# Turning part B's input once in part A and fetching the turned images later: one change to a two-part attention kernel

## Chip, cores and metric

The kernel runs on one core of a Trainium2 chip. The metric is the device time of one execution in microseconds. A core has five engines that run side by side and meet through semaphores: TensorE (PE; its weight loads are shown as PEld), VectorE (DVE), ScalarE (ACT), GpSimd (POOL) and SyncE (SP). SyncE computes nothing here: it issues transfers, one after the other, and a transfer whose semaphore isn't there yet holds up all that stand behind it on SyncE. GpSimd issues some transfers as well. All transfers are carried out by the core's 16 DMA engines.

## What is computed

Two independent parts, both bf16, whose outputs stand side by side in the last dimension. Part A is a sliding attention in which each token looks at 8 tokens, 2 apart. Part B is a recurrence over 64 segments of 32 tokens: each segment attends over 8 memory rows and its own 32 rows, and the first 8 rows of its output are the memory of the next.

```python
def _A_ref(x, wqkv, wo):                    # x (1, 2048, 640), H = 32, Dh = 20
    qkv = (x @ wqkv).reshape(B, S, 3, H, Dh)
    idx = pos[:, None] - arange(8) * 2      # masked where < 0
    logits = einsum('bhsd,bhswd->bhsw', q, k[idx]) * Dh ** -0.5
    o = einsum('bhsw,bhswd->bhsd', softmax(logits), v[idx])
    return o.reshape(B, S, D) @ wo

def _B_ref(x, mem0, Wq, Wk, Wv, Wo, seg_len):   # x (1, 2048, 640), H = 32, Dh = 192, M = 8
    mem = mem0
    for s in range(64):
        h = concatenate([mem, x[:, 32 * s:32 * s + 32]], axis=1)    # 40 rows
        q, k, v = h @ Wq, h @ Wk, h @ Wv                            # per head
        p = softmax(where(mask, q k^T * Dh ** -0.5, -1e9))
        o = einsum('bhte,hed->btd', p v, Wo)
        mem = o[:, :8]
        outs.append(o[:, 8:])
    return concatenate(outs, axis=1)
```

## The kernel before

The two parts run one after the other on TensorE. While part A computes, SyncE loads and copies what part B will need.

**Part A** (`part_a`, L24) works in blocks of 512 tokens for the projections and of 256 tokens for the attention. `turn_x(s)` (L47) lets a transposing transfer lay the s-th block of 512 tokens into `xT`, of which there are two buffers: the transfers for blocks 0 and 1 start at once, block 2 needs the buffer of block 0, block 3 that of block 1. `step(b, fill)` (L178) does the attention of a 256-token block; the projections of the next 512-token block are woven into it (`more`, `group`). Steps 2 and 3 project block 2, steps 4 and 5 block 3. The order of TensorE, VectorE and ScalarE is written out by hand in part A (`manual_schedule`, L234); for SyncE and GpSimd the compiler's scheduler places the instructions, by and large in the order of the text. `output` (L166) stores a result by way of two `ob` buffers, from GpSimd for the first two blocks and from SyncE for the rest (L176). `turn_x(3)` stands at the end of step 1 in the text (L229).

**The loads ahead** (`emit_loads`, L358) are issued by SyncE within part A, in this order: `turn_x(1)`; 37 pieces of part B's weights that stay on the chip (`load_resident`, L326, 320 or 384 KB each); `turn_x(2)`; 23 pieces that don't fit and are copied from their input into a contiguous DRAM tile each (`copy_streamed`, L295); and the copies of x into windows (`copy_windows`, L339).

**The windows.** A segment's TensorE input is 64 columns wide: 32 main columns (8 of memory, which are written over later, and the segment's first 24 tokens), and 32 columns "ahead", the last 8 tokens of each of four segments. `XW` (L337) is a DRAM tile of 64 windows of 64 rows of 640 values, so each token row is copied into the right windows: 26 transfers. In part B `load_x(s)` (L425) turns window s by one transposing transfer into `HX` (128 partitions x 5 x 64), one of two buffers.

**Part B** (`part_b`, L272; `segment`, L594) goes through four groups of 8 heads: projections q, k, v (`project32`, L435), scores, softmax, mixing with v, and the output projection `project_out` (L570). `get_unit` (L387) hands out a weight piece: a resident one, or a streamed one, for which SyncE issues a load from the DRAM copy into one of five `ws` buffers (shown as `t`). Each segment streams the same 23 pieces, in the order k0 (2), k1 (2), v0 (2), k2 (2), v1 (1), o0 (2), k3 (2), v2 (1), o1 (3), v3 (1), o2 (2), o3 (3). Nine further resident pieces (`early`) are loaded when part A frees their memory, and the last 15 (`wait`) when segment 0 first asks for them. At the end of a segment `memory_rows` (L582) writes the new memory into the first columns of the next HX. TensorE's order in part B is written by hand (L655), SyncE's is the scheduler's.

## Time and profile before

Three runs took 2023.1, 2030.83 and 2033.13 us; the median is 2030.83. The profiled execution is one more.

| What | Value |
|---|---|
| profiled execution, its time | 2024.66 us |
| its span, first to last instruction | 2022.8 us |
| part A, until TensorE's first work for part B | 0 to 176.3 us |
| segment 0 | 176.3 to 217 us |
| segments 1 to 62, by the memory rows | 28.6 us each in the mean |
| TensorE busy, 217 to 1990 us | 1727.68 of 1773.00 us |
| DMA share, 0 to 100 us; 100 to 145; 145 to 180; 180 to 217 | 1.02; 0.22; 0.57; 0.98 |
| HX, transposing load | 64 issues, median 1.2 us of SyncE, 4.4 us to landing |
| streamed pieces | 64 x 23 loads, 4.3 to 4.8 us to landing |

How to read it: an engine's line gives the microseconds in which it was busy, merged; "idle before, releaser" says how long it stood and what ended the wait. A matmul's end is modelled, so a TensorE that is shown busy may still be waiting a little. SyncE's instructions are issues; what is told of them is the start, the time that SyncE was held, and the time to landing. The granted clock is the share of TensorE's full speed; 0.5 means that it ran at half speed. The DMA share is the part of the 16 engines' time that packets took, and can lie a little over 1.

### The profile page before, as it was taken

The numbers are of one execution on the slowest core, as the hardware profiler recorded it, in microseconds if no ns is written. First come the engines' busy times: TensorE is split into PE (matmuls) and PEld (weight loads), VectorE is DVE, ScalarE is ACT, GpSimd is POOL, SyncE is SP. The second block draws the span as 40 slices with busy tenths as digits, with TensorE's granted clock in tenths as the row PEclk, the third lists the DMA queues.
The fourth block names the chain that finished last, engine by engine and source line by source line (L and its number), as shares of the span: only waits on it lengthen the run. The fifth ranks groups of instructions, "written<-read, shape, count | busy, mean of one in ns | idle before, by whom it ended". The sixth has DMA issues, their size and how long they took to land.

```text
span 2022.8 us, 97144 instructions
## 1 busy us (share of the span) xinstructions
PE 1945.4 (96%) x42512; PEld 1243.6 (61%) x42512; DVE 1128.3 (56%) x3622; ACT 725.6 (36%) x2126; POOL 193.6 (10%) x674
## 2 busy tenths in 40 slices
PE   7989999999999999999999999999999999999998
PEld 4656666666666666666666666666666665666665
DVE  5875555555555455555555555555555554555554
ACT  3543333333333333333333333333333333333333
POOL 2000000110001101001001001101001001110110
PEclk9999999999999999999999999999999999999999
DMA  9927999999899999999999989999899988989997
GB/s 343 311 76 269 311 300 305 301 302 307 290 305 304 299 288 312 302 304 303 303 299 297 308 292 311 305 303 299 296 298 303 298 304 284 303 293 300 305 302 257
DMA packets 270123, 596.29 MB, mean 295 GB/s; under 512 B 61065, under 2 KB 72841, under 8 KB 269385
## 3 DMA queue, kind: packets, MB, share of 16 engines
q1 hardware_dynamic: 264770, 585.97, 87.9%
q8 instruction: 333, 5.46, 1.1%
q0 software_dynamic: 4928, 4.11, 0.6%
q14 instruction: 92, 0.75, 0.1%
HBM read 576.85 MB, written 18.87 MB: 295 GB/s over the span
## 4 chain that ended last, share of the span: by engine, by line
PE 71%; DMA 19%; DVE 6%; ACT 1%; issue 1%; SPq 1%; POOL 0%; DVEq 0%; POOLq 0%; ACTq 0%
PE acc L443 33%; PE Y L578 18%; DMA t<-wcopy_k 8%; DMA t<-wcopy_o 6%; PE pt L456 6%; PE Sps L515 4%; PE OTps L564 4%; PE pq L95 2%; PE pt L547 2%; DVE sb L423 2%; DMA out_dram<-row 2%; DMA t<-wcopy_v 1%; PE po L161 1%; DMA wcopy_o<-in_B_Wo_dram 1%; PE py L172 1%
## 5 line engine op out<-in xcount | busy, mean ns | idle before, releaser
L443 PEld LDWEIGHTS <-HX 128*32 128x32 bf16 x19380 | 462.7, 96 | 274.3 <-issue 46.5
L578 PEld LDWEIGHTS <-OT 128*64 128x64 bf16 x6144 | 316.8, 109 | 131.0 <-ACT OT L423 20.0
L578 PE MATMUL Y<-wres_o,OT 128*64 128x320 bf16 x3584 | 344.3, 302 | 2.2
L443 PE MATMUL acc<-wres_q,HX 128*32 128x384 bf16 x6460 | 332.6, 328 | 0.5 <-ACT sb L423 0.2
L443 PE MATMUL acc<-t,HX 128*32 128x384 bf16 x4200 | 309.1, 328 | 12.9 <-DMA t<-wcopy_k 10.1
L578 PE MATMUL Y<-t,OT 128*64 128x320 bf16 x2560 | 277.7, 303 | 10.0 <-DMA t<-wcopy_o 9.2
L423 DVE CAST sb<-acc 128x384 bf16<-128x384 f32 x322 | 178.8, 556 | 186.6 <-PE acc L443 171.3
L443 PE MATMUL acc<-wres_v,HX 128*32 128x384 bf16 x4844 | 276.5, 328 | 0.1
L528 ACT ACTIVATE t<-t 128x160 f32<-128x160 f32 x256 | 86.1, 336 | 439.4 <-DVE t L527 439.4
L443 PE MATMUL acc<-wres_k,HX 128*32 128x384 bf16 x3876 | 224.8, 327 | 0.3 <-issue 0.3
L522 DVE SCALAR_TENSOR_TENSOR t<-Sps,mask 128x160 f32<-128x160 f32 x256 | 82.8, 323 | 214.6 <-PE Sps L515 186.6
L423 ACT CAST sb<-acc 128x384 bf16<-128x384 f32 x324 | 153.6, 474 | 125.1 <-PE acc L443 123.5
L456 PE MATMUL pt<-ident,sb 128*128 128x128 bf16 x1938 | 179.4, 221 | 6.9 <-DVE sb L423 1.7
L423 DVE CAST OT<-OTps 128x120 bf16<-128x120 f32 x512 | 125.5, 271 | 97.4 <-PE OTps L564 96.8
L488 POOL COPY QT<-Lb 128x96 bf16<-128x96 bf16 x252 | 67.4, 267 | 1112.0 <-PE Sps L515 955.2
L456 PEld LDWEIGHTS <-sb 128*128 128x128 bf16 x1938 | 110.2, 97 | 82.3 <-issue 32.3
L515 PEld LDWEIGHTS <-QT 128*64 128x64 bf16 (+1 forms) x4096 | 118.9, 109 | 55.1 <-issue 40.5
L423 ACT CAST OT<-OTps 128x120 bf16<-128x120 f32 x512 | 106.0, 258 | 110.7 <-PE OTps L564 110.4
L515 PE MATMUL Sps<-KT,QT 128*64 128x40 bf16 (+1 forms) x4096 | 137.0, 188 | 2.2 <-DVE KT L423 1.0
L530 DVE TENSOR_REDUCE sm<-t 128x4 f32<-128x160 f32 x256 | 81.8, 320 | 78.7 <-ACT t L528 78.7
L564 PEld LDWEIGHTS <-Vst 32*128 32x128 bf16 (+1 forms) x4096 | 62.2, 97 | 82.3 <-issue 60.5
L564 PE MATMUL OTps<-PT,Vst 32*128 32x40 bf16 (+1 forms) x4096 | 109.7, 192 | 0.0
(75 smaller groups left out, 1916.0 us busy)
## 6 DMA issues: line engine op xcount, KB each, us to landing
t<-wcopy_o SPq DMA_DIRECT2D x640, 320.0 KB, 4.3
t<-wcopy_k SPq DMA_DIRECT2D x512, 384.0 KB, 4.8
t<-wcopy_v SPq DMA_DIRECT2D x320, 384.0 KB, 4.8
wres_q<-in_B_Wq_dram SPq DMA_DIRECT2D x20, 384.0 KB, 7.7
wres_v<-in_B_Wv_dram SPq DMA_DIRECT2D x15, 384.0 KB, 7.8
wres_k<-in_B_Wk_dram SPq DMA_DIRECT2D x12, 384.0 KB, 7.7
wres_o<-in_B_Wo_dram SPq DMA_DIRECT2D x14, 320.0 KB, 6.7
wcopy_o<-in_B_Wo_dram SPq DMA_DIRECT2D x10, 320.0 KB, 8.1
```

What stands on the lines that cost most here:

```text
L95: nc.tensor.matmul(pq[32 * d:32 * d + 32], lhsT=wcol[:, k, t, 4 * c + d, :], rhs=xTs[s][:, k, :], start=(k == 0), stop=(k == 4), tile_posi ...
L423: (nc.scalar.copy if copies["n"] % 2 else nc.vector.tensor_copy)(dst, src)
L443: nc.tensor.matmul(ps[n][32 * j:32 * j + 32, :], lhsT=X[:, dc, :], rhs=w[:, 384 * j:384 * j + 384], start=(dc == 0), stop=(dc == 4), tile_ ...
L456: nc.tensor.matmul(pt[:, c], lhsT=sb[:, 128 * c:128 * c + 128], rhs=ident, start=True, stop=True)
L488: nc.gpsimd.tensor_copy(tokens(T)[:, :, 32:L], b[:])
L515: nc.tensor.matmul(Sps[64 * g2:64 * g2 + 64, a, :], lhsT=QT[lo:hi, L * cc:L * cc + 64], rhs=KTt[lo:hi, cc, :], start=(g2 not in seen), sto ...
L522: nc.vector.scalar_tensor_tensor(out=t1[:], in0=Sps[:], scalar=scale, in1=mask[:].unsqueeze(1).to_broadcast([128, 4, L]), op0=ALU.mult, op ...
L528: nc.scalar.activation(t1[:], t1[:], ACTF.Exp)
L530: nc.vector.tensor_reduce(out=sm[:], in_=t1[:], axis=AX.X, op=ALU.add)
L547: nc.tensor.transpose(pt[:, late, :], P[:, late].rearrange("p a n -> p (a n)"), ident)
L564: nc.tensor.matmul(dst, lhsT=V[32 * a:32 * a + 32, e0:e1], rhs=PT[32 * a:32 * a + 32, late, half, :], start=(wide and late == 0 and half = ...
L578: nc.tensor.matmul(Y[64 * gv:64 * gv + 64, :], lhsT=OT[:, L * c:L * c + 64], rhs=w[:, n:n + 320], start=(i == 0 and r == 0), stop=(i == 23 ...
```

## The change

1. The windows are grouped by sets of four segments (`XW` becomes 16 x 64 rows x 4 segments x 640), and all their copies (32 transfers) go to the front of SyncE's queue, right behind `turn_x(1)`.
2. After `turn_x(3)`, at the end of step 1, `rest` issues 16 transposing transfers, each of which turns four windows at once into a stage, and GpSimd stores the stage into four images in DRAM (`XT`, 128 rows of 640 B for each segment). The four stages lie in the memory of the four resident v1 pieces, which are loaded behind that; `copy_streamed` now follows the transposes.
3. `load_x(s)` is a plain load of an image. It moves from the start of `segment` to behind the values of group 1.
4. SyncE's order in part B is that of the text (`manual_schedule` takes SP in).
5. In segment 0, from the sixth streamed piece on, each streamed load is preceded by the load of one of the 15 waiting resident pieces.
6. All outputs of part A are stored by GpSimd.

```diff
-    emit_loads(turn_x)
+    rest = emit_loads(turn_x)
...
-        (nc.sync if b > 1 else nc.gpsimd).dma_start(out2[r0:r0 + 128, 0:D], ob[:])
+        nc.gpsimd.dma_start(out2[r0:r0 + 128, 0:D], ob[:])
...
         if b == 1:
             turn_x(3)
+            rest()
...
-    XW = dpool.tile([n_seg, 2 * SEG, Dm], BF16, name="xwindows")
+    n_sets = n_seg // 4
+    XW = dpool.tile([n_sets, 2 * SEG, 4, Dm], BF16, name="xwindows")
+    XT = dpool.tile([n_seg, 128, 5 * 2 * SEG], BF16, name="ximages")
...
+    def turn_images(stage):
+
+        for b in range(n_sets):
+            part = stage[b % len(stage)]
+            nc.sync.dma_start_transpose(part, XW[b].rearrange("n s d -> n (s d)"))
+            nc.gpsimd.dma_start(XT[4 * b:4 * b + 4].rearrange("s p n -> p s n"),
+                                part.rearrange("p (s c) n -> p s (c n)", s=4))
+
     def emit_loads(turn_x):
         turn_x(1)
-        load_resident(resident[:n_pre], [nc.sync])
+        copy_windows()
+        last = [u for u in resident[:n_pre] if u[:2] == ("v", 1)]
+        load_resident([u for u in resident[:n_pre] if u not in last], [nc.sync])
         turn_x(2)
-        copy_streamed()
-        copy_windows()
+
+        def rest():
+            wide = joined["v", 1][0][:].rearrange("p n c -> p (n c)")
+            turn_images([wide[:, 1280 * i:1280 * i + 1280].rearrange("p (c n) -> p c n", n=2 * SEG) for i in range(4)])
+            copy_streamed()
+            load_resident(last, [nc.sync])
+
+        return rest
...
+    ahead_of = []
+
     def get_unit(u):
...
+        if wait:
+            ahead_of.append(u)
+            if len(ahead_of) > nbuf:
+                v = next(v for v in resident if v in wait)
+                wait.remove(v)
+                load_resident([v], [nc.sync])
         t = wstream.tile([128, SLOT], BF16, tag="ws")
...
     def load_x(s):
         if s < n_seg:
-            nc.sync.dma_start_transpose(HXs[s % 2][:], XW[s])
+            nc.sync.dma_start(HXs[s % 2][:].rearrange("p c n -> p (c n)"), XT[s])
...
     def segment(s):
         last = s + 1 == n_seg
-        load_x(s + 1)
...
         V[1] = values(s, 1)
+        load_x(s + 1)
...
-    with tc.manual_schedule(engines={mybir.EngineType.PE}):
+    with tc.manual_schedule(engines={mybir.EngineType.PE, mybir.EngineType.SP}):
```

More of the change, by code (lines that the diff above doesn't have):

```diff
@@ L320, in unit_tile @@
         return v.rearrange("p (k d) -> p k d", k=2) if u[0] == "o" else v
+    joined = {("v", 1): []}
     def place_resident(pool, units):
         for u in units:
-            res[u] = pool.tile([128, unit_cols(u)], BF16, name="wres_%s%d_%d" % u)[:]
+            part = joined.get(u[:2])
+            if part is None:
+                res[u] = pool.tile([128, unit_cols(u)], BF16, name="wres_%s%d_%d" % u)[:]
+                continue
+            if not part:
+                n = sum(v[:2] == u[:2] for v in units)
+                part.append(pool.tile([128, n, 1536], BF16, name="wres_%s%d" % u[:2]))
+            res[u] = part[0][:, sum(v[:2] == u[:2] for v in res), :]
     def load_resident(units, engs):
@@ L336, in part_b @@
     dpool = ctx.enter_context(tc.tile_pool(name="b_copy", bufs=1, space=bass.MemoryType.DRAM))
-    XW = dpool.tile([n_seg, 2 * SEG, Dm], BF16, name="xwindows")
+    n_sets = n_seg // 4
+    XW = dpool.tile([n_sets, 2 * SEG, 4, Dm], BF16, name="xwindows")
+    XT = dpool.tile([n_seg, 128, 5 * 2 * SEG], BF16, name="ximages")
     def copy_windows():
-        rows = [(XW[0, 0:M], mem2[0:M]), (XW[0, M:SEG], x2[0:SEG - M])]
-        for a, b in ((1, 49), (49, n_seg)):
-            rows.append((XW[a:b, 0:SEG], x2[SEG * a - M:SEG * b - M].rearrange("(s n) d -> s n d", n=SEG)))
-        groups = x2.rearrange("(t n) d -> t n d", n=SEG)[:, SEG - M:SEG]
-        groups = groups.rearrange("(m k) n d -> k m n d", k=4)
-        windows = XW[:].rearrange("(m k) n d -> k m n d", k=4)
-        for r in range(4):
+        rows = [(XW[0, 0:M, 0], mem2[0:M]), (XW[0, M:SEG, 0], x2[0:SEG - M])]
+        sets = x2.rearrange("(m r n) d -> r m n d", r=4, n=SEG)
+        for r in range(4):
+            lo = 1 if r == 0 else 0
+            own = x2[4 * SEG * lo + SEG * r - M:]
+            span = 4 * SEG * (n_sets - 1 - lo)
+            rows.append((XW[lo:n_sets - 1, 0:SEG, r],
+                         own[0:span].rearrange("(m q) d -> m q d", q=4 * SEG)[:, 0:SEG]))
+            rows.append((XW[n_sets - 1, 0:SEG, r], own[span:span + SEG]))
@@ L348, in copy_windows @@
             for i in range(4):
-                dst = windows[r][:, SEG + M * i:SEG + M * i + M]
+                dst, src = XW[:, SEG + M * i:SEG + M * i + M, r], sets[i][:, SEG - M:SEG]
                 if i >= r:
-                    rows.append((dst, groups[i]))
+                    rows.append((dst, src))
                 else:
-                    rows.append((dst[0:n_seg // 4 - 1], groups[i][1:n_seg // 4]))
-                    rows.append((dst[n_seg // 4 - 1], groups[i][n_seg // 4 - 1]))
+                    rows.append((dst[0:n_sets - 1], src[1:n_sets]))
+                    rows.append((dst[n_sets - 1], src[n_sets - 1]))
```

## The prediction

> **What bounds the kernel now.** I read the page's totals and slices first, then who waits for whom, then SyncE's queue in part A, then the microseconds around one transposing load in part B.

> ```profile
> span 2022.8 us, 97144 instructions
> PE 1945.4 (96%) x42512; PEld 1243.6 (61%) x42512; DVE 1128.3 (56%) x3622; ACT 725.6 (36%) x2126; POOL 193.6 (10%) x674
> DMA  9927999999899999999999989999899988989997
> ```

> TensorE is busy for 96% and the DMA engines for 0.9 nearly everywhere; the hole in the third and fourth slices (101 to 202 us) is the second half of part A. So TensorE sets the time, and what can be won is its idle time and what it loses when it restarts. The waits of TensorE:

> ```profile
> PE acc L443 <- DMA t<-wcopy_k: 10.1, 32, 0.9
> PE Y L578 <- DMA t<-wcopy_o: 9.2, 23, 0.8
> PE pt L547 <- DVE P L540: 6.1, 23, 0.7
> PE pq L95 <- DMA xT<-in_A_x_dram: 5.9, 1, 5.9
> PE acc L443 <- DMA t<-wcopy_v: 1.1, 4, 0.4
> ```

> (us in total, times, longest.) 20.4 us in 59 waits go to streamed weights over the whole of part B (21.5 us in 70, where waits of 60 to 150 ns are counted too), and 5.9 us to one late transpose in part A. A matmul of L443 takes 328 ns (the page's group) and the next is issued 41 ns later (20 in 0.82 us), so a wait that shows as idle has hidden some 0.28 us more while the pipeline drained: 59 x 0.28 = 16.5, in all 37 us. Segments run 27.8 to 31.2 us, 28.6 in the mean.

> SyncE's queue in part A (start, duration) and the restart of TensorE:

> ```profile
> 16.00 3.88 SPq L328 DMA_DIRECT2D wres_q<-in_B_Wq_dram  x5
> 48.08 1.32 SPq L328 DMA_DIRECT2D wres_q<-in_B_Wq_dram  x2
> 50.13 6.59 SPq L49 DMA_TRANSPOSE xT<-in_A_x_dram  x1
> 82.34 24.57 SPq L356 DMA_DIRECT2D xwindows<-in_B_x_dram  x25
> 107.02 2.98 SPq L49 DMA_TRANSPOSE xT<-in_A_x_dram  x1
> ```
> ```profile
> 70.19 1.09 PE L95 MATMUL pq<-xT,a_wq 128*32 128x512 bf16 x16
> 112.15 2.37 PE L95 MATMUL pq<-xT,a_wq 128*32 128x512 bf16 x20 [5.89 <-DMA xT<-in_A_x_dram]
> ```

> The four blocks of A's x (L49) are turned by SyncE. The fourth is issued at 107.0 only because 25 window copies stand ahead of it, and TensorE stands for it. The third, issued at 50.1 behind the resident pieces, is in time: its first use is the line at 70.19.

> Around the load of HX at 1009.25 (columns: busy and count of each engine, granted clock, DMA share, GB/s):

> ```profile
> 1010.00:1011.00 1.00, 1.00 (x16) 0.48 (x10) 0.24 (x1) 0.00 (x0) 0.12 (x1) 1.00 0.97 370
> 1011.00:1012.00 1.00, 1.00 (x48) 0.55 (x44) 0.29 (x2) 0.27 (x2) 0.00 (x0) 1.00 0.78 239
> 1012.00:1013.00 1.00, 1.00 (x22) 0.74 (x16) 0.18 (x1) 0.15 (x1) 0.00 (x0) 1.00 1.35 123
> 1013.00:1014.00 1.00, 0.90 (x14) 0.55 (x10) 0.00 (x0) 0.00 (x0) 0.00 (x0) 1.00 0.49 115
> ```

> While the transpose runs, the stream falls from about 300 to 120 GB/s. Averaged over the segments' loads it is 215 and 164 GB/s in the third and fourth us after the issue: (85 + 136) KB missing, 0.74 us of stream a segment. It hits the k pieces with which the next segment begins.

> **The sum, part by part.**

> *Transposing load out, plain load in.* Removed: 64 transposes, 1.2 us of SyncE each (median row) and the 0.74 us of stream. Added: 128 rows of 640 B; packets of 640 B took 32 to 35 ns in part A, 128/16 x 34 ns = 0.27 us. The k waits it causes are those in the first 7 us of a segment: 16 waits, 3.8 us, with the drain 3.8 + 16 x 0.28 = 8.3. I take them as gone. The out_dram rows of a segment travel in the same first microseconds, when the stream catches up at 350 to 360 GB/s, and VectorE waits for them (14.6 us, 12 times), which passes to TensorE as part of the 6.1 us above: I take 2 of it. Against that, the 0.27 us now lie between v1 and o0, some 8 us ahead of k3, the tightest place (26 waits, 8.1 us, at 14 to 17 us into the segment). At worst every such segment moves by 0.27, 26 x 0.27 = 7; SyncE is waiting for free slots there, so I take 1.3. Body: -8.3 - 2 + 1.3 = **-9**, bounds +7 (no gain, full price) and -37 (every stream wait goes with it).

> *Windows first in part A, two transposes.* The fourth block no longer waits for the windows: -5.9, and -1.4 for the 2.9 us of work at half clock that follow (granted clock 0.50 from 112.2 to 115): -7.3. The third block now stands behind 32 window copies instead of none, and behind 33 resident pieces instead of 37. Pieces go at 0.98 us (37 from 16.0 to 50.1, less a short start). Window copies: 15 of them took 0.75 us each once nothing held them (95.6 to 106.9), the median issue is 0.56; the DMA time of 4096 rows of 1280 B at 62 ns is 4096/16 x 62 = 16 us. So 16 to 24, I take 21. The block's packets start at 16 + 21 + 33 x 0.98 = 69.3 and need 4 us to land: 73.3 against 70.2, a stall of 3.1 and 1 us of half clock: +4, bounds 0 and +8. Sum for A: **-3.3**.

> *Sixteen transposes and stores.* On the DMA engines: 1280 packets of 256 B at 20.7 ns, 1.66 us each, 26.5 in all; stores of 512 packets of 640 B, 1.1 each, 17.4. Room: the share was 0.22 from 100 to 145 and 0.57 from 145 to 180, so 35 + 15 = 50 us are free for 44. On SyncE one costs some 2 us (1.19 for 320 packets, 2.98 for 2560). A stage is reused after transpose and store: 4 to land, 1 to issue, 5 to 6 to land (out_dram from POOL at 80 us: 5.8), over four stages 2.6 us each: 80 + 16 x 2.6 = 122. Then 23 streamed copies (56.8 to 81.2 before: 24 us), 4 v1 pieces, HX and 9 early pieces, 14 us: done by about 160, and part B begins near 173. Cost nothing; the cover is 13 us, and without it each us late is a us of TensorE.

> *Outputs of A to POOL.* 12 issues of 0.54 us. SyncE waited 50.5 us for ScalarE's ob; now POOL does, and the image stores behind it. Two ob buffers give a step (18 us) of grace: nothing.

> *SyncE in program order; pieces ahead in segment 0.* Around 1009 to 1037 SyncE already issues the 23 pieces in program order: nothing. From 180 to 217 the DMA share is 0.98, but TensorE waits 1.1 us there in all. Fifteen pieces of 1 us placed earlier: -1.1 to +3, I take **-0.5**.

> Sum: -9 - 3.3 - 0.5 = -12.8. The profiled execution took 2024.66 us (span 2022.8, 1.9 around it); it would become 2011.9. It lies 6.2 under the median of the three runs, 2030.83, from which I count: **2018**.

> **Rivals.**

> *The tail of part A is late (slower).* One mechanism: the four stages. If transposes land as under backlog (10.2 us, the third block) and stores at 8.5 (POOL at 63 us), one takes (10.2 + 1 + 8.5)/4 = 4.9 us, 16 take 79: done at 159, the streamed copies at 183, HX and the first k after 188 to 197 instead of 173: +15 to +24, with the body's -9 and A's -3.3 about 2030.8 + 19.5 - 12 = **2038**. It decides from (173 - 38 - 80)/16 = 3.4 us per transpose. For it: stores may queue on POOL behind outputs. Against it: the engines are free there, and outputs of 160 KB landed in 1.8 us after 120.
> VectorE's products in part A take 1.22 us each, and POOL's issues beside them 0.54 us with 5.8 us to land at 80 us; whether any of that is VectorE's doing can't be told from the full queue. [...]

> *The ring of five slots is the limit (same).* k0's slot is freed by o14 of the segment before; if the late k pieces come from that and not from the transpose, the waits at 14 to 17 and at 26 us stay and the first ones too, and only A's -3.3 and a little remain: **2027**. For it: 54 of the 70 waits lie more than 7 us into a segment. Against it: the fall to 120 GB/s.

> *All stream waits are one chain (faster).* If the catching up is what makes the later pieces late as well, 37 us go: **1992**. For it: after the fall the stream runs at 350 to 400 GB/s, with no reserve. Against it: by 8 us into the segment it is back at 300.

> **How the numbers follow.** Chances: my forecast 0.42, all waits 0.15, the ring 0.20, the late tail 0.23. Less than 0.5% (10 us) can't be told from no change, since the three runs span 10 us. The forecast's own range is 2008 to 2026, of which I put 0.30 beyond 10 us and 0.12 within; of the ring 0.03 faster, 0.15 same and 0.02 slower; of the tail 0.21 slower, 0.02 same; all waits is faster. So faster 0.48, same 0.29, slower 0.23. The range reaches into both outer cases, 1994 to 2046: it leaves out about half of all waits and a fourth of the tail.

> **What would show it.** Right: no wait of L95 for xT at 112; no fall of GB/s in the last 6 us of a segment; waits for wcopy_k in the first 7 us gone, segments of 28.5 us in the mean. Wrong: a wait of L95 near 70 of over 8 us; SyncE still in its transposes after 135, or L443 waiting at its first matmuls; k3's waits grown by more than the first ones shrank; or a stream that still falls at the plain load.

## The result, and the profile after

The changed kernel takes 2044.59 us (median of six runs, 2043.22 to 2056.21); the kernel before, timed beside it, 2027.12 (six runs, 2017.82 to 2033.13). The ratio is 1.0105 with a 95% interval of 1.0068 to 1.0141: slower by about 1%. The profiled execution took 2044.17 us, its span is 2042.4, 19.6 more than before.

| What | Before | After | Difference |
|---|---|---|---|
| span | 2022.8 | 2042.4 | +19.6 |
| TensorE's first work for part B | 176.3 | 193.4 | +17.1 |
| first memory rows (end of segment 0) | 217.2 | 235.3 | +18.1 |
| segments 1 to 62, mean of one | 28.601 | 28.597 | 0.00 |

So 17.1 of the 19.6 us are lost in part A; segment 0 adds 1.0, and the end behind the last memory rows 1.8. The segments, for which the change was forecast to win 9 us, show no difference. (The mean of one profile is uncertain by about 0.1 us a segment: in e4 below, which leaves part B as it was before, it is 28.72.) The page's totals and slices after:

```profile
span 2042.4 us, 97154 instructions
PE 1948.3 (95%) x42512; PEld 1248.8 (61%) x42512; DVE 1127.1 (55%) x3622; ACT 726.8 (36%) x2126; POOL 212.0 (10%) x702
DMA  8995999999999998999999989989989998989997
```

The hole of the DMA engines, two slices before (101 to 202 us), is now the fourth slice alone (153 to 204): the new transposes fill most of it, as they should. TensorE is busy for 2.9 us more and idle for some 17 more. Its waits (us in total, times, longest):

```profile
PE pq L95 <- DMA xT<-in_A_x_dram: 10.3, 1, 10.3
PE Y L616 <- DMA t<-wcopy_o: 9.6, 22, 2.2
...
PE py L172 <- ACT ob L174: 7.9, 1, 7.9
PE acc L481 <- DMA t<-wcopy_k: 7.4, 15, 1.4
...
PE acc L481 <- DMA t<-wcopy_v: 4.5, 10, 1.0
```

The wait for xT has not gone, it has become longer; a wait of 7.9 us is new; the streamed weights come to 21.5 us, 20.4 before. Both long waits, in TensorE's timeline:

```profile
72.07 0.39 PE L145 MATMUL pr<-P,a_repm 32*128 32x512 bf16 x2
82.79 1.51 PE L95 MATMUL pq<-xT,a_wq 128*32 128x512 bf16 x12 [10.33 <-DMA xT<-in_A_x_dram]
...
139.33 1.49 PE L172 MATMUL py<-a_wo,ao 128*128 128x320 bf16 x5 [7.93 <-ACT ob L174]
```

**The first wait** is for the third block of A's x. SyncE's timeline (start, how long SyncE was held, how many) shows what stood ahead of it:

```profile
16.65 0.86 SPq L370 DMA_DIRECT2D xwindows<-in_B_mem_dram  x1
17.56 25.28 SPq L370 DMA_DIRECT2D xwindows<-in_B_x_dram  x31
42.88 2.48 SPq L338 DMA_DIRECT2D wres_q<-in_B_Wq_dram  x5
...
72.12 1.21 SPq L338 DMA_DIRECT2D wres_q<-in_B_Wq_dram  x2
74.05 9.35 SPq L49 DMA_TRANSPOSE xT<-in_A_x_dram  x2
83.44 6.61 SPq L376 DMA_TRANSPOSE wres_v<-xwindows  x4
```

The windows hold SyncE for 26.2 us (16.65 to 42.84), the 33 pieces until 73.3, and only at 74.05 is the third block's transpose issued. Even then most of its packets don't start: the pieces were issued ahead of the engines (the one of 72.1 lands at 79.3), and the block's own packets, a few from 77.5 on, go mostly from 80 to 82.7.

**The second wait** is for an output buffer. GpSimd's and ScalarE's timelines:

```profile
130.86 0.75 POOL L377 DMA_DIRECT2D ximages<-wres_v  x1 [1.77 <-DMA wres_v<-xwindows]
131.61 1.10 POOL L176 DMA_DIRECT2D out_dram<-ob  x2
139.90 0.54 POOL L176 DMA_DIRECT2D out_dram<-ob  x1 [7.20 <-ACT ob L174]
```
```profile
138.85 1.08 ACT L174 CAST ob<-py 128x320 bf16<-128x320 f32 x3 [8.34 <-DMA out_dram<-ob]
```

The two results of block 2 lay ready in their buffers at 113.9 and 115.2. The scheduler had put their stores behind the last image store on GpSimd, and an image store waits for its transpose (50.6 us in 13 waits between 84 and 142). So they were issued at 131.6 and 132.2, and the first landed at 138.8; until then ScalarE had no buffer for block 3, and TensorE no place for its next product.

**Half clock after each.** In windows around the two waits (length; busy and count of PE, PEld, DVE, ACT, POOL; granted clock; DMA share; GB/s) the clock stays at half speed when the matmuls run again:

```profile
72.00:83.00 11.00, 0.67 (x8) 0.43 (x10) 3.08 (x3) 1.66 (x5) 0.00 (x0) 0.61 1.13 287
83.00:88.00 5.00, 5.00 (x46) 1.88 (x42) 1.23 (x1) 1.66 (x3) 0.00 (x0) 0.50 1.16 223
139.00:142.70 3.70, 3.37 (x17) 1.93 (x20) 0.13 (x1) 1.50 (x5) 1.08 (x2) 0.51 1.04 327
```

It is at half from 74.4 to 88.0 and from 135.8 to 142.7. Work at half takes twice as long (the 20 matmuls of L95 take 2.36 us from 82.8 and 1.25 us from 88.3), so (88.0 - 82.8)/2 = 2.6 and (142.7 - 139.3)/2 = 1.7 us are lost. Part A then adds up: 10.3 + 2.6 + 7.9 + 1.7 = 22.5, less the 7.3 of the fourth block's old stall, plus 2.2 that were lost ahead of 72 us (0.8 in the start, 1.4 because a stretch at half clock from 33.4 us lasted 6.8 us where it was 3.4): 17.4, where 17.1 were measured.

**Part B.** The fall of the stream that the prediction saw is gone. The four microseconds before segment 28, at the place of the transposing load before:

```profile
998.00:999.00 1.00, 1.00 (x44) 0.64 (x46) 0.00 (x0) 0.29 (x1) 0.12 (x1) 1.00 0.99 296
999.00:1000.00 1.00, 1.00 (x20) 0.56 (x22) 0.47 (x2) 0.42 (x2) 0.00 (x0) 1.00 0.85 280
1000.00:1001.00 1.00, 1.00 (x18) 0.84 (x16) 0.00 (x0) 0.00 (x0) 0.00 (x0) 1.00 0.93 273
1001.00:1002.00 1.00, 0.92 (x16) 0.26 (x12) 0.16 (x1) 0.43 (x1) 0.00 (x0) 1.00 0.96 336
```

273 to 336 GB/s, where it fell to 115. Over all segments the two lowest microseconds rose from 225 and 136 GB/s to 260 and 301. Yet the waits for weights in the first 7 us of a segment are 3.5 us in 12, from 3.8 in 16. The stream is smoother and the pieces are as late as they were, only in other places. Of the waits over 150 ns, those for k in the first 7 us fell from 2.6 us in 9 to 1.0 in 3 and those for v there rose from 0.7 in 3 to 2.2 in 6. For o0, which now comes right behind the plain load (7 to 14 us into a segment), they rose from 0.7 us in 2 to 5.4 in 9, and for k3 (14 to 18 us) they fell from 7.5 in 23 to 4.3 in 9.

### The profile page after: what moved, and what is told of

It is laid out like the page before. It is cut to its first block, busy times and chain, and to the rows that moved or that the text cites. A ratio compares the mean times of both kernels' runs of the same rounds, so it can differ in the third digit from the quotient of the medians.

```text
span 2042.4 us, 97154 instructions
## 1 busy us (share of the span) xinstructions
PE 1948.3 (95%) x42512; PEld 1248.8 (61%) x42512; DVE 1127.1 (55%) x3622; ACT 726.8 (36%) x2126; POOL 212.0 (10%) x702
## 4 chain that ended last, share of the span: by engine, by line
PE 69%; DMA 20%; DVE 6%; SPq 2%; issue 2%; ACT 1%; POOL 0%; DVEq 0%; POOLq 0%; ACTq 0%
PE acc L481 32%; PE Y L616 19%; DMA t<-wcopy_o 7%; PE pt L494 6%; DMA t<-wcopy_k 5%; PE Sps L553 4%; PE OTps L602 4%; DMA out_dram<-row 2%; PE pt L585 2%; DMA t<-wcopy_v 2%; DVE sb L461 2%; DMA wres_v<-xwindows 1%; SPq L370 1%; SPq L49 1%; DMA ximages<-wres_v 1%
## 5 line engine op out<-in xcount | busy, mean ns | idle before, releaser
L481 PEld LDWEIGHTS <-HX 128*32 128x32 bf16 x19380 | 463.2, 96 | 272.7 <-issue 46.0
L616 PEld LDWEIGHTS <-OT 128*64 128x64 bf16 x6144 | 321.0, 109 | 130.1 <-issue 21.2
L481 PE MATMUL acc<-wres_q,HX 128*32 128x384 bf16 x6460 | 332.5, 328 | 0.5 <-ACT sb L461 0.3
L481 PE MATMUL acc<-t,HX 128*32 128x384 bf16 x4200 | 309.3, 328 | 13.6 <-DMA t<-wcopy_k 7.4
L481 PE MATMUL acc<-wres_v,HX 128*32 128x384 bf16 x4844 | 277.1, 328 | 0.6 <-issue 0.5
L481 PE MATMUL acc<-wres_k,HX 128*32 128x384 bf16 x3876 | 223.6, 326 | 0.0
```

The costliest lines, as they stand in the source:

```text
L481: nc.tensor.matmul(ps[n][32 * j:32 * j + 32, :], lhsT=X[:, dc, :], rhs=w[:, 384 * j:384 * j + 384], start=(dc == 0), stop=(dc == 4), tile_ ...
L616: nc.tensor.matmul(Y[64 * gv:64 * gv + 64, :], lhsT=OT[:, L * c:L * c + 64], rhs=w[:, n:n + 320], start=(i == 0 and r == 0), stop=(i == 23 ...
```

## The experiments

Three questions were open. Are the two stalls of part A the whole loss, each worth its own length, or does a removed stall only bring out the next late thing? Why did part B win nothing, although its disturbance is gone: is the load of HX cheap because the stream had slack, or does the new load cost as much as the old? And what does make the weight pieces late? Each kernel was timed against the kernel before on the same chip; since that one's median differed between chips (2026.7 to 2034.9 us), ratios to it are compared, not times.

### Third block ahead of the pieces (e1_x2_first, from the changed kernel)

```diff
         copy_windows()
+        turn_x(2)
         last = [...]
         load_resident([u for u in resident[:n_pre] if u not in last], [nc.sync])
-        turn_x(2)
```

> The changed kernel with the third block of A's x turned right behind the window copies instead of behind the 33 resident pieces. Theory S (the two new stalls of part A are separate): the 10.3 us wait of L95 for xT goes and the 7.9 us wait of L172 for ob stays, so some 11.5 us less with the half clock, 2033 us. Theory C (one chain: the image stores on GpSimd end at 131 us whatever TensorE does, and the outputs of A stand behind them): the wait for xT goes, the wait for ob grows by as much, to 17 to 20 us, and the time stays at 2045 within 4 us.

Measured: 2036.87 us, ratio 1.0034 (1.0009 to 1.0059). The wait for xT is gone, but two others stand in TensorE's list:

```profile
PE acc L481 <- DMA t<-wcopy_k: 14.5, 22, 5.9
...
PE py L172 <- ACT ob L174: 3.5, 1, 3.5
```

What changed on GpSimd:

```profile
101.22 0.54 POOL L176 DMA_DIRECT2D out_dram<-ob  x1 [16.79 <-ACT ob L174]
...
103.07 3.00 POOL L377 DMA_DIRECT2D ximages<-wres_v  x4
```

This time the scheduler put block 2's results ahead of the image stores. GpSimd waited for ScalarE until 101.2, and four image stores that were due stood behind it; SyncE's transposes, whose four stages they free, stood still from 91 to 106. So part A ended earlier, but the streamed copies and HX were late (HX issued at 166.5, the first k pieces from 175.9, where TensorE could have begun at about 177), and 5.9 us were paid there. Neither expectation was met: the stall goes at its price, and what the same mixed queue on GpSimd holds up next depends on where the scheduler puts the results.

### Outputs issued by ScalarE (e2_out_act), and both edits (e3_both)

```diff
-        nc.gpsimd.dma_start(out2[r0:r0 + 128, 0:D], ob[:])
+        nc.scalar.dma_start(out2[r0:r0 + 128, 0:D], ob[:])
```

> The changed kernel with the outputs of part A issued by ScalarE instead of GpSimd, so that they no longer stand behind the image stores. Both theories: the 7.9 us wait of L172 goes, 9 us less with its half clock, 2035.5 us; the wait for xT at 72 us stays at 10.3. If part B's start were held by SyncE's queue (image stores, streamed copies, early pieces done late), TensorE would wait in its first matmuls of L481 instead, up to the same 8 us, and the time would stay near 2044.

> Both edits in the changed kernel. Theories S and C alike: both waits gone, part A ends near 173 us instead of 194, 2024 us, that is 3 us under the kernel before (the fourth block's 5.9 us and its half clock, less ScalarE's issues), if part B's segments cost the same in both kernels. If the transposing load costs 9 us in part B, as I forecast, it would come out at 2015. If SyncE's queue is late for part B, 2030 or more, with waits in the first matmuls of L481.

Measured: 2089.91 us, ratio 1.0288 (1.0270 to 1.0306), and for both edits 2066.67, 1.0178 (1.0149 to 1.0208). These failed as experiments: SyncE's window copies came to wait for an output transfer that ScalarE issues (33.6 us in one wait in e2, 33.9 in e3). In e2 the windows lasted until 77.5 and the wait for xT was 43.6 us. The edit added a dependence of its own, so nothing follows for the theories.

### Image stores on SyncE (e10_stores_sp), and without the early third block (e12_stores_only)

```diff
+        def store(b):
+            nc.sync.dma_start(XT[4 * b:4 * b + 4]..., stage[b % len(stage)]...)
...
             nc.sync.dma_start_transpose(part, XW[b]...)
-            nc.gpsimd.dma_start(XT[4 * b:4 * b + 4]..., part...)
+            if b >= 2:
+                store(b - 2)
+        store(n_sets - 2)
+        store(n_sets - 1)
```

e10 also has the edit of e1; e12 has this one alone.

> The changed kernel with the third block turned behind the window copies and the image stores issued by SyncE, each two transposes behind its own, so that GpSimd has only the outputs of part A. Theory C (the second wait is GpSimd's queue, in which outputs and image stores stand in each other's way): no wait for ob, none for xT, 18 us and two half clocks less than the changed kernel, 2024 us or a little under. If the tail of part A is late all the same, waits in the first matmuls of L481 and 2028 to 2035. If only the third block matters, 2033 as forecast for the first experiment by theory S.

> The changed kernel with the image stores issued by SyncE, the third block where the change has it. Theory C: the wait for ob goes, the wait of L95 for xT stays at 10.3 us; 10.3 and a half clock of 1 to 1.4 above the kernel with both edits (2025), 2036. If the two stalls were one (the second only because the first shifted TensorE against the stores): no wait for ob and none for xT, 2025.

Measured: e10 2025.21 us, ratio 0.9998 (0.9983 to 1.0012). Neither long wait of part A is left. Transposes and stores lie between 82.4 and 129.2, part A is done at 171.4, the first memory rows come at 215.0 (235.3 in the changed kernel, 20.3 later). With both stalls out, the loss is out: 1.0105 against 0.9998, whose intervals don't meet.

Something new comes out at the head of part B. The first k pieces are issued only at 166.8, behind everything that moved ahead of them, and TensorE now waits in segment 0 for a resident v piece and for k (the longest wait of the k line):

```profile
166.77 3.58 SPq L438 DMA_DIRECT2D t<-wcopy_k  x4
```
```profile
PE acc L487 <- DMA t<-wcopy_k: 6.2, 18, 1.1
...
PE acc L487 <- DMA wres_v<-in_B_Wv_dram: 1.1, 1, 1.1
```

Part A ends 4.9 us earlier than before, but from there to the first memory rows it takes 43.6 us where it took 40.9, so 2.2 are left.

e12: 2039.27 us, ratio 1.0009 (0.9984 to 1.0034). Its profile is as expected, no wait for ob and this one for xT:

```profile
PE pq L95 <- DMA xT<-in_A_x_dram: 9.6, 1, 9.6
```

and its first memory rows come 13.7 us after those of e10. But in the times the two differ by 0.0011 in the ratio, some 2 us, with an uncertainty of about 6, or by 5.9 us in the medians less their own before. The medians as they are, 2039.27 and 2025.21, lie 14.1 us apart, as the traces do; it is the kernel before, 8.1 us slower on e12's chip than on e10's, that takes most of this away. So the stall is plain in the trace, and what it is worth in time was not settled.

### Copies and windows behind the fourth block (e4_copies_late, from the kernel before)

```diff
             turn_x(3)
+            rest()
...
         turn_x(2)
-        copy_streamed()
-        copy_windows()
+
+        def rest():
+            copy_streamed()
+            copy_windows()
+
+        return rest
```

> The kernel before with one edit: streamed copies and window copies are issued behind the fourth block's transpose (at the end of step 1) instead of ahead of it. No images, the transposing load stays. If the fourth block was late only because of its place in SyncE's queue: the 5.9 us wait goes with its half clock, 7.3 us less, 2020 us. Rival: the copies then end at about 125 us and something of part B's first loads becomes late: 2024 to 2030.

Measured: 2020.9 us, ratio 0.9947 (0.9929 to 0.9966), the lowest ratio of the kernels here that compute all. Its only aim is the old stall of the fourth block, which is now issued in time:

```profile
73.38 6.01 SPq L49 DMA_TRANSPOSE xT<-in_A_x_dram  x1
```

There is no wait for xT, and the first memory rows come at 210.7, 6.5 earlier than before. The segments take 28.72 us in this profile, 0.12 longer each than in the profile before, which uses the 6.5 up there (span 2024.0 us); the gain rests on the timed runs. The gain of part A that the change was forecast to bring is there to be had, by moving the copies back instead of the windows forward.

### No load of x after the second window (e5_no_x_load, from before; e7_image_no_load, from the changed kernel)

```diff
-        if s < n_seg:
+        if s < 2:
```

Both leave the windows of segments 2 to 63 unloaded, so those segments compute on old x.

> The kernel before without the transposing load of HX from segment 2 on (left out: segments 2 to 63 work on the main and ahead columns of segments 0 and 1). Theory T (the transposing load costs part B some 9 us, as I forecast): a segment 28.46 us instead of 28.60, 2018 us beside 2027. Theory R (the stream has time to catch up, and segments wait for other reasons): a segment unchanged within 0.05 us, 2025 to 2029.

> The changed kernel without the plain load of HX from segment 2 on (left out: segments 2 to 63 work on the main and ahead columns of segments 0 and 1). If the plain image load costs the body as much as the transposing one did, 0.1 us a segment: 2044.6 - 7 = 2038. If it is free: 2042 to 2047, and the body of the changed kernel would be at the one without loads already. Part A is untouched: waits of 10 us for xT and 8 us for ob.

Measured: e5 2019.25 us, ratio 0.9972 (0.9952 to 0.9992): all 62 transposing loads together are worth 5.7 us (1.6 to 9.7), 0.1 us a segment; segments take 28.49 us. e7 2048.83, ratio 1.0064 (1.0039 to 1.0089): against the changed kernel's 1.0105, the plain loads are worth about 8 us, give or take 9. This is no clean price either, for e7's part A was not left as expected: GpSimd has the same order, but the transposes ran later, and the wait for ob is twice as long.

```profile
PE py L172 <- ACT ob L174: 17.2, 2, 15.7
```

So the 7.9 us of the changed kernel's profile are the figure of one execution. By segments, 28.54 us against 28.60, e7's loads are worth 0.06 us each. The old load, with its fall of the stream, costs about as little as the new one.

### Loading twice (e6_x_load_twice, e6b_twice_in_order, from before; e13_image_at_start, e14_image_twice, from e10)

```diff
             nc.sync.dma_start_transpose(HXs[s % 2][:], XW[s])
+            nc.sync.dma_start_transpose(again[:], XW[s])
```

`again` is a tile that nothing reads. e6b also keeps SyncE in the order of the text. e14 has the same for the plain load; e13 moves the single plain load back to the start of a segment.

> The kernel before with each transposing load issued twice, the second time into a tile that nobody reads. Theory T: another 0.74 us of stream a segment and another 9 us, 2036. Theory R: the stream catches up with one more, 2027 to 2030; only from there does a third of the first microseconds' reserve run out.

> The kernel before with SyncE's order in part B that of the text (as in the change) and each transposing load issued twice, in its place, the second time into a tile that nobody reads. The unordered trial let the second loads run ahead in a bunch between 147 and 422 us and cost 1.1 us each there. If a transposing load costs part B 0.1 us a segment (the whole removal gave 0.11 in segment means), this one gives the same again: 2027 + 7 = 2034. If it costs its 0.74 us of stream: 2027 + 46 = 2073. If the stream catches up wholly: 2027.

> The changed kernel with SyncE's stores and the early third block (2025 us, no stall in part A), and the plain load of the image back at the start of the segment, where the transposing load was. If the plain load gained nothing because its new place, ahead of o0 and k3, cost what the transpose had cost at the old one: segments of 28.50 us or less in the mean, 2017. If the place doesn't matter: segments of 28.6 to 28.7 as with all five earlier versions, 2025.

> The same kernel with each image loaded twice in the middle of the segment, the second time into a tile that nobody reads. A second transposing load cost 0.8 to 0.9 us a segment. If the price goes by the stream's lost time (0.27 us of packets, no fall beside it) and the stream is at its edge: 0.27 us a segment at most, 17 us, 2042. If the ring takes it: 0.1 us a segment like the first, 2031, or nothing, 2025.

Measured: e6 2099.38, ratio 1.0371 (1.0343 to 1.0399), but it is no clean test: the scheduler drew the 64 second loads together between 147 and 422 us. e6b 2092.85, ratio 1.0264 (1.0226 to 1.0302), with each second load behind its first:

```profile
1016.16 1.18 SPq L428 DMA_TRANSPOSE HX<-xwindows  x1
1017.39 1.25 SPq L429 DMA_TRANSPOSE again<-xwindows  x1
```
```profile
PE acc L445 <- DMA t<-wcopy_k: 42.2, 74, 2.6
```

The second transpose costs 53 us, 0.83 a segment, nearly all in k pieces 1 to 7 us into a segment; that is close to the 0.74 us of stream that the prediction worked out for one. The first, by e5, costs 0.1. That fits a stream with the reserve to make up for one transpose in a segment, and not for two, so that the price was sized well and put on the wrong load. A second transpose at another place in the segment was not tried.

e13: 2029.39 us, ratio 0.9991 (0.9975 to 1.0008); e14: 2029.34, ratio 1.0003 (0.9987 to 1.0019). Neither the place of the plain load nor a second one makes a difference that shows: e13 less e10, 1.4 us less, and e14 less e10, 1.0 us more, each give or take 4.5 and on different chips; e14 less e13, on the same chip and with both edits between them, 2.4, give or take 4.7. Segments take 28.73 us in both profiles. The waits do go with the load: at the start of the segment (e13) there are 4.5 us in 8 for k in the first 7 us and 0.4 in 1 for o0; with the load in the middle (e10) 0.4 in 2 and 3.4 in 8.

### A sixth buffer (e8_ring6, from before; e11_copies_ring6, from e4)

```diff
-    ... nbuf=5,
+    ... nbuf=6,
+    resident.remove(("o", 10, 0))
...
+    res["o", 10, 0] = res["o", 9, 0]
```

The memory for the sixth buffer is that of the resident piece o10. e8 doesn't load o10 and multiplies by o9 in its place; e11 streams one o piece more instead, 24 a segment, and computes all.

> The kernel before with six streaming buffers instead of five. To make room piece 10 of the output projection isn't loaded and piece 9 stands in for it (left out: one resident load of 320 KB, 1 us of DMA in segment 0). If five slots are what makes the stream late (theory R in the form of the forecast's rival): the 21 us of stream waits and their drains, 37 us in all, shrink to a third, 2000 to 2006. If late pieces come from slow transfers that a sixth slot can't cover, or if the engines' bandwidth is the limit: under 8 us, 2019 to 2027.

> A version to beat both: the kernel before with the copies behind the fourth block's transpose, and six streaming buffers instead of five, for which piece 12 of the output projection becomes a streamed one (24 a segment, 320 KB more). Six buffers gave 18 us with 23 pieces, the copies 10. If 24 pieces leave the ring's gain alone: 2000. If the extra 0.9 us of DMA a segment takes half of it: 2010. If the stream's bandwidth is then the limit: 2020 or more, with waits for t all over the segment.

Measured: e8 2006.89 us, ratio 0.9911 (0.9891 to 0.9932): 18 us, with the transposing load in place (a piece is 0.98 us on SyncE, so the load left out is about 1 us of it). The waits for weights fall from 20.4 us in 59 to 3.1 in 6, and this is what is left of them:

```profile
PE acc L445 <- DMA t<-wcopy_v: 1.6, 2, 0.9
PE acc L445 <- DMA t<-wcopy_k: 1.5, 4, 0.5
```

The 21 to 27 us that the expectation reckoned, with the drains, were not reached. Between the first and the last memory rows TensorE is busy 8.9 us less, 0.17 for each wait that went where 0.28 had been taken, and its waits for VectorE grew from 7.6 us in 26 to 16.2 in 50.

e11: 2027.43, ratio 0.9957 (0.9935 to 0.9980), no better than e4 alone (0.9947). In the profile the waits for weights are half of e4's, 12.6 us against 25.8, yet the segments take 28.72 us in both; TensorE's waits for VectorE are 13.5 us in the segments against 8.8. A 24th piece takes, by an estimate from 320 KB at the 370 GB/s of the microsecond from 1010 before the change, 0.9 us more of the DMA engines in each segment; that this is what takes the buffer's gain was not shown.

## Why the prediction was wrong

It said 2018 us and faster; it became 2044.6 and slower. In the profiled executions the forecast was -12.8 and the outcome +19.5, 32.3 apart. By steps: part A 20.4 (third block 8.9, outputs 9.6, its start 2.2; 0.3 too much together), segment 0 1.5, the body 8.7, the end behind the last memory rows 1.6.

**The third block, "+4, bounds 0 and +8": 10.3 and 2.6 of half clock, 12.9.** The mechanism was right, the size beyond its bound. Three numbers were too small. The windows took 26.2 us, not 21 (16 to 24 had been allowed): 32 at 0.82 us, where 0.56 to 0.75 had been read from the old queue. "Packets start at 69.3" counted SyncE's issues at 0.98 us each as if the engines kept up with them; SyncE was done with the pieces at 73.3, but one issued at 72.1 landed at 79.3, and the block, issued at 74.05, landed some 8.7 us later and not 4. And half clock cost 2.6 us, not 1. e1 took back the move of this one block, and its wait was gone.

**"Outputs of A to POOL ... Two `ob` buffers give a step (18 us) of grace: nothing": 7.9 and 1.7.** The image stores were said to wait behind the outputs; what was not followed was the reverse, the outputs behind 16 image stores, each of which waits for a transpose. 18 us of grace were counted against one wait, and the results were held from 113.9 to 131.6 and then took 7.2 to land, 25 us in all. On SyncE they had not stood behind any image store, for there were none. e10 and e12, which take the image stores out of GpSimd's queue, have no such wait; e7, with the same order on GpSimd, has one of 15.7.
Before the change TensorE waited for an output buffer only 0.2 us in all; what the move cost, 7.9 us, came of the queue in which the results had to wait.

**The body, "-9": 0.** The load of HX did disturb the stream, the fall is gone as forecast, and a transpose does cost 0.83 us a segment when it is one too many (e6b). What failed is "I take them as gone", with all else as it was: waits that stand just behind an event were booked as its price. (They were not all for k, either: 9 of the 12 that are over 150 ns were, the others for v.) Those for k did shrink, and waits for v and o0 came in their place. With the load left out altogether the waits for weights are 20.3 us, from 20.4, and 0.1 us a segment is gained (e5); with a sixth buffer they go although the load stays (e8). So in the segments it was the rival of the ring of five slots that held; I had given it 0.20, and its count, 54 of 70 waits more than 7 us into a segment, was better evidence than the fall of GB/s. The plain load between v1 and o0, for which +1.3 was taken, draws waits to o0, but shows no price of its own in the time (e13, e14).

**The slower rival** had the sign, not the mechanism. The sixteen transposes took 43 us, 2.7 each where 2.6 was forecast; with a start at 83.4 they end at 126.5, the streamed copies at 145.5, HX is issued at 150.7, all before TensorE needs them. The image stores landed in 5.1 us in the median (3.9 to 7.2), no later than the 5 to 6 that were reckoned, beside products of VectorE of 1.22 us each; whether VectorE has a part in their time was not tried. But the changed kernel's part A is 17 us longer than before, and that is cover. Where the stalls are out, a late tail does come: the first k pieces are waited for 5.9 us in e1, where GpSimd held the stores up, and 1.1, 2.9 and 7.1 us in e10, e13 and e14, where SyncE issues them. "Done by about 160" was too early: in e10 the first k pieces are issued at 166.8.

**Right.** The fourth block's old stall, -7.3: e4 has it alone, and in its profile the first memory rows come 6.5 us earlier (by its ratio it wins 11 us, 7 to 14). The price of the sixteen transposes and stores on SyncE and on the DMA engines was nothing in the changed kernel, where the stalls covered them; what they cost there came by way of GpSimd's queue.

**Segment 0, "-0.5": +1.0.** The 1.1 us of waits that the fifteen pieces were to save had been read from 176 to 300 us; segment 0 itself had no wait over 150 ns for a transfer before, and has 0.6 us of them after. What lengthens it beyond that was not found.

What stays open is what the third block's stall is worth in time (13.7 us between the traces of e12 and e10, some 2 by their ratios), and why the second stall is 7.9 us in one execution and 15.7 in another.

## What to carry to other kernels

When a step is moved into an in-order queue, list what will stand behind it and ask of each when its owner needs it, in both directions, and add to the issues the backlog that the DMA engines still have behind them (here some 6 us). A wait that follows an event is not that event's price: take the event away, or double it, before its removal is costed, since a stream with slack can pay little for one disturbance (0.1 us a segment here) and nearly all of it for a second (0.83). Where late pieces are spread over the whole period, look at the number of buffers first (a sixth was worth 18 us in e8).

## What the runs showed of the hardware

A transfer that ScalarE issued held SyncE's copies for 33.6 us, in a kernel where no data passes between them (e2). Whether the semaphore or the scheduler's order ties them was not tried.
